# A two-layer transformer on one core: VectorE's exponential from three shifted bit patterns, layer 1's late queries projected in place, another order of its first row blocks

## The chip, the core and the metric

One core of a Trainium2 chip runs the program. It has a matrix engine (TensorE, PE in the profile; its weight loads are PEld), VectorE (DVE), ScalarE (ACT), GpSimd (POOL), and a queue that starts transfers (SyncE, SP). The engines run side by side, each takes its own instructions in order, and they wait for each other by semaphores. Only TensorE, VectorE and ScalarE reach PSUM, the memory into which matmuls write. The metric is the device time of one execution in microseconds; a kernel's time is the median of its runs.

## The reference, cut to what matters

2048 rows of 448 numbers pass twice through the same two blocks, with the same weights: attention with 16 heads of 28, then a hidden layer of 1792 with a squared ReLU.

```python
x = x + A(layernorm(x), wqkv, wo)
x = x + B(layernorm(x), w1, b1, w2, b2)
x = x + A(layernorm(x), wqkv, wo)
x = x + B(layernorm(x), w1, b1, w2, b2)

# A: q, k, v of 16 heads of 28
scores = einsum("bhqd,bhkd->bhqk", q, k) * 28 ** -0.5
o = einsum("bhqk,bhkd->bhqd", softmax(scores), v);  return o @ wo
# B
h = x @ w1 + b1;  r = where(h > 0, h, 0);  return (r * r) @ w2 + b2
```

Softmax needs an exponential for each of 2 x 16 x 2048 x 2048 scores, and its sums come with the product P x V through columns of ones in V.

## The kernel before, in words

**Tiling.** A *unit* is 128 keys' worth of partitions by 512 columns of scores of one head: two key blocks of 128 against a row block of 256 queries (in the last two row blocks four against 128). There are 1024 units in a layer. Four heads make a head group g (four groups), and the eight row blocks (layer 1: nine, the last two of 128 rows) are numbered from 0. A *pass* is one row block, one head group and a range of key blocks; the lists `OPENING` and, in layer 1, `CUTS` and `AHEAD` say in which order passes come.

**Three engines share the exponentials.** TensorE writes scores (L1157) into one of two PSUM tiles of three banks. ScalarE takes all three units of such a tile in one exponential of 128x1536 (L1195), or only two, 128x1024, while VectorE takes the third (`a_unit`, L1219 or L1217). Scores come out scaled so that a unit's value is log2 of the exponential times 128, which is how a bf16 number's bits are spaced. VectorE therefore makes an int16 number out of the score and calls it bits of a bf16 number. In `a_rest` three more operations with constants bend it to the exponential: `bent` (L1266, int16), `half` (L1272, low bytes to f16) and `whole` (L1277, high bytes back in place); the planner gives each to GpSimd or VectorE. `close` (L1281, VectorE) multiplies two of them. The result is the sum of two tiles, `z` and `x2`, and both are multiplied by V on TensorE and added in PSUM (L1383 for `z` and ScalarE's units, L1348 for `x2`). Where much is queued on GpSimd (`PLIM`), another form runs on VectorE alone (`a_whole`, L1235, L1239, L1242).

**Buffers.** ScalarE's results go into a ring of twelve tiles `pt`; VectorE's unit lies in such a tile or in a *cell*: `v_c`, or parts of K, V of a layer that hold nothing yet or nothing more (in rows: `v_c`, `K_sb`, `V_sb`, `h`). Two small PSUM banks (`R_m`) serve everything else: projections, the accumulator of P x V, the hidden layer.

**Order.** The program is written by a `Planner`. Streams (scores, exponentials, P x V, each row block's chain of work) offer their next operation; the planner keeps a clock for each engine, with a duration for each operation, and issues what can start first, by priority. `PACE` holds settings that take effect from the numbered exponential on (`BUSY`, `TB`, `LAG` and so on say when VectorE may take a unit; `HEAT` when a filler matmul, L1644, is put on TensorE); `FORCE` and `SKIP` name exponentials at which VectorE must, or must not, take a unit.

**A row block's chain** (`chain`): output projection, addition to x (L1516), statistics (L651), normalisation (L775), transposes (L715), hidden layer in TensorE (all these projections are L812), ReLU (L1587) and square (L1594), second product, addition (L1516). In layer 0 it goes on to layer 1's keys, values and queries (`qkv`): K of the first two head groups, V, K of the other two, and at once Q (copies from PSUM: L835, L863, L831). In layer 1 the block is stored.

## Time and profile before

| | |
|---|---|
| three runs | 802.92, 803.11, 803.15 us; median 803.11 |
| the profiled execution | span 801.1 us from the first to the last instruction; its page gives no other time of its own |
| instructions | 29158; TensorE 12205 matmuls, VectorE 1836, ScalarE 702, GpSimd 703 |
| ScalarE's exponentials | 683: 344 of 1536 columns, 339 of 1024 |
| opening, exponentials, closing | 0 to 9.3, to 786.5, to 801.1 us |

A row of a group reads: line, engine, operation, written tile <- read tiles, shapes, count | busy time in us, mean duration of one in ns | idle time of the engine just before them, and who ended it. A row of a stretch reads: from:to, its length, then for each engine busy us and instructions, the granted TensorE clock (1.00 is full), the share of the DMA engines, GB/s. A row of the line of time or of the chain reads: start, us, engine, what; a merged row can hold both shapes of a line. A row of waits reads: who waited <- for whom: us in total, times, longest. Busy time of TensorE is modelled, so a busy TensorE is not one at its peak.

### The profile page before, as it was taken

To read this page: it belongs to the slowest core of one execution; us is meant where nothing else is said; L and a number is where in the kernel's file an instruction comes from. 1 tells how busy PE (TensorE), PEld (TensorE's weight loads), DVE (VectorE), ACT (ScalarE), POOL (GpSimd) and SP (SyncE) were. 2 spreads that over 40 slices of the span, in tenths; PEclk is the share of its full clock that TensorE was granted. 3 is DMA by queue.
4 is the path that set the end of the run, shared out by engine and by line. 5 is a ranking of instruction groups with operands and counts; after the bars stand their busy time and mean duration, and the time that the engine had idled before them with its cause. 6 is when DMAs were issued, how large, how long until landed. Compare 5 with 4: busy or idle time off the path is not lost.

```text
span 801.1 us, 29158 instructions
## 1 busy us (share of the span) xinstructions
PE 777.5 (97%) x12205; PEld 417.1 (52%) x12205; DVE 749.9 (94%) x1836; ACT 788.9 (98%) x702; POOL 445.3 (56%) x703
## 2 busy tenths in 40 slices
PE   9999989999999999999999999989999999999998
PEld 6555545544554545555454545445454554445666
DVE  8999999999999999999999998999999999999754
ACT  8999999999999999999999999999999999999995
POOL 3346777657676664544566667767655656533200
PEclk9999999999999999999999999999999999999999
DMA  9200010000000000000000000011100000000000
GB/s 254 82 2 2 4 34 25 17 16 16 17 3 16 16 16 16 3 17 15 2 3 2 2 2 2 12 35 30 32 12 22 21 23 21 27 11 21 22 15 19
DMA packets 32481, 18.13 MB, mean 23 GB/s; under 512 B 17819, under 2 KB 31900, under 8 KB 32349
## 3 DMA queue, kind: packets, MB, share of 16 engines
q1 hardware_dynamic: 32204, 16.16, 7.4%
q8 instruction: 95, 1.56, 0.8%
q14 instruction: 38, 0.30, 0.1%
q10 hardware_dynamic: 144, 0.11, 0.0%
HBM read 13.98 MB, written 2.06 MB: 20 GB/s over the span
## 4 chain that ended last, share of the span: by engine, by line
PE 38%; ACT 36%; DVE 17%; issue 9%; POOL 0%; DMA 0%; ACTq 0%; DVEq 0%
ACT pt L1195 36%; PE mt L812 17%; PE sc L1157 11%; PE oT L1383 6%; DVE pt L1219 2%; DVE r L1587 2%; PE oT L1348 1%; DVE pt L1217 1%; DVE x_sb L1516 1%; DVE st L651 1%; DVE K_sb L1281 1%; DVE v_c L1281 1%; DVE V_sb L1594 1%; DVE oTn L1507 1%; DVE v_c L1219 1%
## 5 line engine op out<-in xcount | busy, mean ns | idle before, releaser
L1195 ACT ACTIVATE pt<-sc 128x1536 bf16<-128x1536 f32 (+1 forms) x683 | 776.1, 1287 | 1.4 <-PE sc L1157 1.1
L1157 PE MATMUL sc<-Q_sb,K_sb 32*128 32x256 bf16 (+1 forms) x4606 | 278.5, 265 | 16.9 <-ACT pt L1195 13.3
L1157 PEld LDWEIGHTS <-K_sb 32*128 32x128 bf16 x4606 | 100.0, 92 | 188.2 <-issue 119.7
L1383 PE MATMUL oT<-pt,V_sb 128*32 128x256 bf16 (+1 forms) x3974 | 168.0, 268 | 0.6 <-DVE Q_sb L831 0.3
L1383 PEld LDWEIGHTS <-V_sb 128*32 128x32 bf16 x4352 | 101.6, 96 | 45.0 <-issue 36.0
L812 PE MATMUL mt<-xnT,w 128*128 128x256 bf16 (+1 forms) x904 | 119.3, 270 | 0.4 <-DVE x_sb L1516 0.2
L1277 POOL TENSOR_SCALAR pt<-pt 128x512 int16<-128x512 int8 x124 | 79.0, 640 | 42.9 <-ACT pt L1195 5.2
L812 PEld LDWEIGHTS <-w 128*128 128x128 bf16 x952 | 78.0, 98 | 34.2 <-issue 25.1
L1219 DVE TENSOR_SCALAR pt<-sc 128x512 int16<-128x512 f32 x128 | 87.3, 685 | 1.9 <-PE sc L1157 1.4
L1587 DVE TENSOR_SCALAR r<-mt 128x512 bf16<-128x512 f32 (+1 forms) x107 | 73.0, 682 | 3.0 <-PE mt L812 2.3
L676 POOL TENSOR_TENSOR rstd<-mv,mhalf 128x2 f32<-128x2 f32 (+1 forms) x34 | 25.4, 747 | 85.1 <-DVE mv L679 58.0
L812 PE MATMUL mt<-w,V_sb 128*128 128x448 bf16 (+2 forms) x288 | 67.2, 346 | 0.0
L1272 POOL TENSOR_SCALAR v_c<-pt 128x512 f16<-128x512 uint8 x55 | 36.5, 665 | 29.6 <-DVE xnT L727 4.6
L1277 POOL TENSOR_SCALAR v_c<-v_c 128x512 int16<-128x512 int8 x60 | 40.2, 670 | 21.0 <-DVE V_sb L1272 4.3
L1219 DVE TENSOR_SCALAR v_c<-sc 128x512 int16<-128x512 f32 x69 | 46.5, 680 | 0.6 <-PE sc L1157 0.6
L1516 DVE TENSOR_TENSOR x_sb<-x_sb,mt 128x448 bf16<-128x448 bf16 x61 | 37.5, 615 | 8.1 <-PE mt L812 7.8
L651 DVE BATCH_NORM_STATS2 st<-x_sb 128x6 f32<-128x448 bf16 x63 | 38.9, 619 | 0.8 <-DMA x_sb<-in_A_x_dram 0.5
L812 PEld LDWEIGHTS <-V_sb 128*128 128x128 bf16 x302 | 25.0, 98 | 24.1 <-issue 10.0
L1348 PE MATMUL oT<-v_c,V_sb 128*32 128x256 bf16 (+1 forms) x306 | 35.7, 272 | 0.0
L1277 POOL TENSOR_SCALAR K_sb<-K_sb 128x512 int16<-128x512 int8 x41 | 26.5, 647 | 10.8 <-DVE v_c L1281 2.4
L1594 DVE TENSOR_TENSOR V_sb<-r 128x512 bf16<-128x512 bf16 x70 | 29.1, 419 | 3.1 <-ACT r L1585 2.8
L812 PE MATMUL mt<-wo,oTn 128*128 128x448 bf16 x128 | 30.3, 355 | 0.4 <-DVE oTn L1465 0.3
(224 smaller groups left out, 1255.9 us busy)
## 6 DMA issues: line engine op xcount, KB each, us to landing
rec<-scr SPq DMA_DIRECT2D x54, 128.0 KB
out_dram<-x_sb SPq DMA_DIRECT2D x15, 112.0 KB
x_sb<-in_A_x_dram SPq DMA_DIRECT2D x7, 224.0 KB
w<-in_B_w_dram SPq DMA_DIRECT2D x1, 1568.0 KB
w<-in_B_w_dram SPq DMA_DIRECT2D x1, 1344.0 KB
dn<-oT_sb SPq DMA_DIRECT2D x54, 4.0 KB
V_sb<-in_A_wqkv_dram SPq DMA_DIRECT2D x4, 168.0 KB
scr<-dn SPq DMA_DIRECT2D x27, 8.0 KB
```

The lines of the kernel that those rows point to most:

```text
L651: nc.vector.bn_stats(out=box["st"][:, :], in_=x_sb[:, t0 + j, :] if src is None else src())
L812: nc.tensor.matmul(box["t"][:, c0:c0 + n], lhsT=lhsT() if callable(lhsT) else lhsT, rhs=rhs, start=a, stop=b)
L1157: nc.tensor.matmul(dst[k][:, i * nt * P:(i + 1) * nt * P], lhsT=K_sb[l][rows, g, (kb + i) * P:(kb + i + 1) * P], rhs=Q_sb[rows, g, t0 * P: ...
L1195: t = nc.scalar.activation(out=pt[:, 0:n], in_=gbuf[gi]["sc"][:, 0:n], func=AF.Exp, scale=float(np.log(2.0)) * 2.0 ** -FRAC)
L1219: t = nc.vector.tensor_scalar(out=z.bitcast(DT.int16), in0=src, scalar1=2.0, scalar2=EXP_BIAS, op0=ALU.mult, op1=ALU.add)
L1272: on(e).tensor_scalar(out=box["f"], in0=gbuf[gi]["z"].bitcast(DT.uint8).rearrange("p (n t) -> p n t", t=2)[:, :, 0], scalar1=2.0 ** -9, sc ...
L1277: on(e).tensor_scalar(out=gbuf[gi]["z"].bitcast(DT.int16), in0=gbuf[gi]["z"].bitcast(DT.int8).rearrange("p (n t) -> p n t", t=2)[:, :, 1], ...
L1348: nc.tensor.matmul(box["t"][DHP * hh:DHP * hh + DHP, 0:n], lhsT=V_sb[l][:, kb + i, 4 * g + hh, :], rhs=gbuf[gi]["x2"][:, i * n:(i + 1) * n ...
L1383: nc.tensor.matmul(box["t"][DHP * hh:DHP * hh + DHP, 0:n], lhsT=V_sb[l][:, tb, 4 * g + hh, :], rhs=p, start=begin and j < G, stop=close an ...
L1516: nc.vector.tensor_tensor(out=x_sb[:, tb, lo:hi], in0=x_sb[:, tb, lo:hi] if src is None else src[:, lo:hi], in1=t[:, 0:hi - lo], op=ALU.add)
L1587: nc.vector.tensor_scalar(out=r[:, 0:w], in0=t[:, 0:w], scalar1=0.0, scalar2=None, op0=ALU.max)
L1594: nc.vector.tensor_tensor(out=h[:, 0:w // n, :], in0=r, in1=r, op=ALU.mult)
```

## The change

**The exponential.** VectorE's first operation now adds one constant to the score and keeps it from going below zero (L1240 after). That int16 number, read as bf16, is a piecewise linear interpolant of the exponential. Two more come from adding 37 and 84 to the same bits (of 128 to an octave; both are `add`, L1261, on GpSimd or VectorE), and VectorE adds these two up (`close`, L1268). `z` is the first tile as it is, `x2` the sum; both are again multiplied by V. `whole`, the operation in place on `z`, and the form on VectorE alone are gone. The ring buffer or cell of `z` is now given back after three readers: both additions and the matmul.

**Late queries.** For row blocks 4 to 7 of layer 0 (`QDEF`), the normalised transposed rows for layer 1 are kept in the place of Q itself. Their Q projections wait until the last keys of layer 1 are there (`late_queries`), and since they overwrite what they read, no result is copied out before the last of the block's projections has run.

**Order of passes.** `BOUND` takes the place of `CUTS`: row blocks 1 to 3 on keys 0 to 9, then row block 0 on keys 0 to 13 and at once 14 and 15, then row blocks 1 to 3 on the rest. Row block 0 is cut once, as before, only later. In layer 0, `OPENING` cuts row block 1's last range in two, keys 8 to 11 and 12 to 15, which adds one sum of partial results (L1408) for each of four head groups.

**Settings.** `PACE` is another table throughout (two rows are shown), and `FORCE` and `SKIP` are part of it. A group of four units (three for ScalarE, one for VectorE) is possible in the code, but `MFREE` of 5 never allows it.

```diff
+SHIFTS = (37, 84)
+def lines(x, by):
+    x = x + by / 2.0 ** FRAC
+    return 2.0 ** np.floor(x) * (1.0 + x - np.floor(x))
+X = np.arange(0.0, 1.0, 2.0 ** -12)
+EXP_BASE = float((127.0 - np.log2(np.mean(sum(lines(X, s) for s in (0, *SHIFTS)) / 2.0 ** X))) * 2.0 ** FRAC)
...
-OPENING = ((0, 0, 2), (0, 2, 4), (1, 0, 4), (1, 4, 8), (0, 4, 8), (0, 8, 12), (1, 8, 16), (0, 12, 16))
+OPENING = ((0, 0, 2), (0, 2, 4), (1, 0, 4), (1, 4, 8), (0, 4, 8), (0, 8, 12), (1, 8, 12), (0, 12, 16), (1, 12, 16))
...
-CUTS = (0, 10, 16)
+BOUND = ((1, 0, 10), (2, 0, 10), (3, 0, 10), (0, 0, 14), (0, 14, 16), (1, 10, 16), (2, 10, 16), (3, 10, 16))
...
-    440: {'HEAT': 0.6, 'WINDOW': 3.4, 'CHUNK': 2},
+    672: {'CHUNK': 3, 'HEAT': 0.6, 'FORCE': (679,)},
...
+            def late_queries():
+                yield Op("-", 0.0, None, deps=[("K", 1, g, NTB - 1) for g in range(G)])
+                for a in qs:
+                    yield from turned(*a, after=[("qq", t0)])
+                yield Op("-", 0.0, None, deps=[last.deps[0]], sets=("qq", t0))
...
         def take(e):
-                t = nc.vector.tensor_scalar(out=z.bitcast(DT.int16), in0=src, scalar1=2.0, scalar2=EXP_BIAS, op0=ALU.mult, op1=ALU.add)
+            t = nc.vector.tensor_scalar(out=z.bitcast(DT.int16), in0=src, scalar1=EXP_BASE, scalar2=0.0, op0=ALU.add, op1=ALU.max)
+        c.need = 3
...
-        t = Op(("POOL", "DVE"), (EDUR, TDUR), bent, deps=[c], acq=lambda: room_for(unit), sets=("t2", gi), port=True)
-        h = Op(("POOL", "DVE"), (EDUR, 0.42), half, deps=[c], acq=lambda: cell_for(unit), port=True)
-        w = Op(("POOL", "DVE"), (EDUR, 0.42), whole, deps=[t, h], sets=("w", gi), port=True)
-        o = Op("DVE", 0.42, close, deps=[t, h], rel=h, sets=("x", gi), port=True)
+        for k in range(2):
+            o.append(Op(("POOL", "DVE"), (EDUR, TDUR), add(o, k), deps=[c], acq=(lambda: cell_for(unit)) if k else (lambda: room_for(unit)),
+                        rel=z, sets=() if k else ("t2", gi), port=True))
+        o = Op("DVE", 0.42, close, deps=ts, rel=ts[1], sets=("x", gi), port=True)
...
-            xt2 = yield from layernorm(t0, nt, None, mv=mv)
+            xt2 = yield from layernorm(t0, nt, None, mv=mv, place=Q_sb[:, :, t0 * P:t0 * P + n] if qb >= QDEF else None)
```

Three places of the built programs show it. First GpSimd, late in layer 0, from one row block's normalisation (`rstd`) on; before:

```order
L676 TENSOR_TENSOR rstd<-mv,mhalf 128x2
L1266 TENSOR_SCALAR K_sb_103<-pt 128x512
L1272 TENSOR_SCALAR v_c<-pt 128x512
L1277 TENSOR_SCALAR pt<-pt 128x512
L1266 TENSOR_SCALAR K_sb_103<-V_sb_106 128x512
L1272 TENSOR_SCALAR v_c<-V_sb_106 128x512
L1266 TENSOR_SCALAR V_sb_106<-v_c 128x512
L1277 TENSOR_SCALAR V_sb_106<-V_sb_106 128x512
L1277 TENSOR_SCALAR v_c<-v_c 128x512
```

Three operations to a unit. The same place now:

```order
L686 TENSOR_TENSOR rstd<-mv,mhalf 128x2
L866 MEMSET V_sb_106 128x16x4
L1261 TENSOR_SCALAR v_c<-pt 128x512
L1261 TENSOR_SCALAR V_sb_106<-v_c 128x512
L1261 TENSOR_SCALAR v_c<-pt 128x512 x2
L1261 TENSOR_SCALAR V_sb_106<-pt 128x512
L1261 TENSOR_SCALAR K_sb_103<-pt 128x512
L1261 TENSOR_SCALAR v_c<-pt 128x512
L1261 TENSOR_SCALAR V_sb_106<-pt 128x512 x2
```

Two operations to a unit, and none that writes where it reads. Second, VectorE where layer 1's last keys come out of PSUM (K_sb_103 holds layer 1's keys); before:

```order
L835 CAST K_sb_103<-mt 128x2x256
L1242 TENSOR_SCALAR V_sb_105<-V_sb_105 128x512
L1266 TENSOR_SCALAR v_c<-K_sb_102 128x512
L1235 TENSOR_SCALAR K_sb_102<-h 128x512
L1239 TENSOR_TENSOR K_sb_102<-h,K_sb_102 128x512
L1408 TENSOR_TENSOR oT_sb<-oT,K_sb_102 128x256
L1219 TENSOR_SCALAR v_c<-sc 128x512
L1281 TENSOR_TENSOR v_c<-v_c,K_sb_102 128x512
L1219 TENSOR_SCALAR v_c<-sc 128x512 x2
L1242 TENSOR_SCALAR h<-h 128x512
L1219 TENSOR_SCALAR K_sb_102<-sc 128x512
L831 TENSOR_SCALAR Q_sb<-mt 128x2x256
```

The last queries follow the last keys. Now the four late blocks' queries stand in pairs behind all keys; the first two pairs:

```order
L841 TENSOR_SCALAR Q_sb<-mt 128x2x256
L1240 TENSOR_SCALAR v_c<-sc 128x512
L841 TENSOR_SCALAR Q_sb<-mt 128x2x256
L1399 TENSOR_TENSOR oT_sb<-oT,K_sb_102 128x256
L1268 TENSOR_TENSOR v_c<-v_c,K_sb_102 128x512
L1268 TENSOR_TENSOR v_c<-v_c 128x512
L1268 TENSOR_TENSOR V_sb_105<-V_sb_105,v_c 128x512
L1479 RECIPROCAL dn<-dn 128x16
L1261 TENSOR_SCALAR v_c<-v_c 128x512 x2
L1240 TENSOR_SCALAR h<-sc 128x512
L841 TENSOR_SCALAR Q_sb<-mt 128x2x256 x2
```

Eight such copies of queries stand behind the last keys instead of two. Third, VectorE at the end of the program (r and V_sb_105: hidden layer; x_sb: the two last row blocks); before:

```order
L727 COPY xnT<-tp 128x4x128
L1594 TENSOR_TENSOR V_sb_105<-r 128x512 x3
L1516 TENSOR_TENSOR x_sb<-K_sb_102,sc 128x448
L1594 TENSOR_TENSOR V_sb_105<-r 128x256
L1516 TENSOR_TENSOR x_sb<-K_sb_102,mt 128x256
L1516 TENSOR_TENSOR x_sb<-K_sb_102,mt 128x192
```

And now:

```order
L737 COPY xnT<-sc 128x4x128
L1578 TENSOR_SCALAR r<-mt 128x256
L1585 TENSOR_TENSOR V_sb_105<-r 128x512 x3
L1585 TENSOR_TENSOR V_sb_105<-r 128x256
L1507 TENSOR_TENSOR x_sb<-K_sb_102,mt 128x256
L1507 TENSOR_TENSOR x_sb<-K_sb_102,sc 128x192
L1507 TENSOR_TENSOR x_sb<-K_sb_102,sc 128x448
```

The addition of row block 7 (128x448) moved behind the two of row block 8.

284 lines of the change are left out of this document (132 added, 152 removed).

## The prediction

> **What bounds the kernel now.** First the page: how busy each engine is, and whether that holds in every slice.
>
> ```profile
> span 801.1 us, 29158 instructions
> PE 777.5 (97%) x12205; PEld 417.1 (52%) x12205; DVE 749.9 (94%) x1836; ACT 788.9 (98%) x702; POOL 445.3 (56%) x703
> ACT  8999999999999999999999999999999999999995
> POOL 3346777657676664544566667767655656533200
> PEclk9999999999999999999999999999999999999999
> ```
>
> ScalarE (ACT) is busy 98% of the span and in every slice but the last; the granted TensorE clock is full throughout. Second, ScalarE's groups with shapes kept apart, and its line of time at both ends.
>
> ```profile
> L1195 ACT ACTIVATE pt<-sc 128x1536 bf16<-128x1536 f32 x344 | 487.6, 1502 | 0.9 <-PE sc L1157 0.8
> L1195 ACT ACTIVATE pt<-sc 128x1024 bf16<-128x1024 f32 x339 | 337.9, 1069 | 0.5 <-PE sc L1157 0.4
> ```
> ```profile
> 9.32 7.08 ACT L1195 ACTIVATE pt<-sc 128x1536 bf16<-128x1536 f32 x5 [0.25 <-PE sc L1157]
> ...
> 769.12 17.39 ACT L1195 ACTIVATE pt<-sc 128x1536 bf16<-128x1536 f32 x13
> ```
>
> The reader is to see one unbroken row of 683 exponentials from 9.32 to 769.12 + 17.39 = 786.51 us, 777.2 us long, with 0.9 + 0.5 = 1.4 us of idle time ahead of them in all. So the time is 9.3 us of opening, 777.2 us of exponentials back to back, and 14.6 us of closing. Inside the row the one lever is how many exponentials are of the short kind, where VectorE takes the third unit: a long one is 1502 ns and a short one 1069 ns, and the difference, 433 ns, is what a unit costs on ScalarE. Third, the other engines by stage.
>
> ```profile
> core 0: us, PE busy (x) PEld busy (x) DVE busy (x) ACT busy (x) POOL busy (x), PEclk, DMA share, GB/s
> 80.00:120.00 40.00, 38.09 (x580) 20.70 (x572) 38.80 (x91) 40.00 (x37) 29.96 (x47) 1.00 0.08 18
> 512.00:532.00 20.00, 17.48 (x295) 8.34 (x294) 19.52 (x51) 20.00 (x20) 12.19 (x19) 1.00 0.13 31
> 720.00:760.00 40.00, 39.41 (x851) 23.93 (x843) 35.40 (x85) 40.00 (x34) 12.81 (x19) 1.00 0.07 19
> 760.00:786.50 26.50, 26.16 (x626) 16.58 (x614) 14.21 (x36) 26.50 (x21) 1.82 (x2) 1.00 0.09 20
> 786.50:801.10 14.60, 11.53 (x153) 9.38 (x150) 6.45 (x18) 4.94 (x10) 1.67 (x2) 0.98 0.06 17
> ...
> 798.40:801.10 2.70, 0.00 (x0) 0.00 (x0) 0.32 (x1) 0.00 (x0) 0.00 (x0) 0.90 0.15 43
> ```
>
> VectorE is at 97% to 98% in the middle, so it can take more units only if a unit costs it less. In the closing TensorE works 11.53 of 14.6 us, and 2.7 of the other 3.1 lie behind its last matmul: what the change adds to TensorE there is added to the time.
>
> **The change part by part.** Durations are those of the profiled execution, whose span is 801.1 us; the median of the three runs, 803.11 us, lies 2.0 us above it. I add those 2.0 us unchanged.
>
> *The exponential.* The order of the two programs gives the counts. Short exponentials go from 339 to 352, long ones from 344 to 331; together they stay 683. So 13 units leave ScalarE: 13 x 433 ns = 5.6 us. What a unit costs the other two engines:
>
> ```profile
> L1219 DVE TENSOR_SCALAR pt<-sc 128x512 int16<-128x512 f32 x128 | 87.3, 685 | 1.9 <-PE sc L1157 1.4 <-issue 0.2
> L1281 DVE TENSOR_TENSOR v_c<-v_c 128x512 bf16<-128x512 bf16 x58 | 24.3, 420 | 1.1 <-POOL v_c L1272 1.1
> L1266 DVE TENSOR_SCALAR v_c<-pt 128x512 int16<-128x512 int16 x21 | 6.0, 285 | 0.0
> L1277 DVE TENSOR_SCALAR v_c<-v_c 128x512 int16<-128x512 int8 x9 | 3.8, 419 | 0.0
> L1277 POOL TENSOR_SCALAR pt<-pt 128x512 int16<-128x512 int8 x124 | 79.0, 640 | 42.9 <-ACT pt L1195 5.2
> L1266 POOL TENSOR_SCALAR v_c<-pt 128x512 int16<-128x512 int16 x29 | 19.7, 680 | 11.7 <-DVE pt L1219 3.8 <-DVE oTn L1507 2.6 <-DVE V_sb L1594 1.1
> L1408 DVE TENSOR_TENSOR oT_sb<-oT,K_sb 128x256 f32<-128x256 f32 x20 | 8.3, 416 | 0.3 <-PE oT L1383 0.2
> ...
> L1348 PE MATMUL oT<-v_c,V_sb 128*32 128x256 bf16 x294 | 34.9, 274 | 0.0
> ```
>
> Every new operation has a row of its own form already: the conversion from PSUM (685 ns), the add of a constant in int16 (285 ns on VectorE, 680 on GpSimd), the closing sum (as the product, 420). VectorE: conversions and closings go from 338 to 351, 13 x (685 + 420) = +14.4 us; int16 constants on VectorE from 124 + 68 + 68 = 260 to 211, 49 x 285 = -14.0; the byte forms, 46 x 419 = -19.3, are gone; partial sums of P x V go from 37 to 41 (row block 1's new cut in layer 0), 4 x 416 = +1.7. Sum -17 us of 749.9. GpSimd: 640 operations at 640 to 680 ns become 491 at 680, some 640 x 650 - 491 x 680 = -82 us of 445.3. TensorE: 13 more units have a second tile to multiply with V, two 256-column matmuls of 274 ns each, 7.1 us even if none ran beside another, spread over the whole span; and 30 filler matmuls (31 before, one now) go. All of this lies beside the exponentials, so I cost it at nothing. Its cover is the row of exponentials itself; should a conversion come late, the next scores can't be written and ScalarE waits, and that is priced below.
>
> *Layer 1's late queries and the new order of row blocks.* The projections are the same in number and size (1366 matmuls of 256 columns and 721 of 448 in both orders), only later, and no DMA is added or moved past another. For row blocks 4 to 7 the evacuation of the first pair of head groups waits on VectorE for the last matmul of the second, and behind it in VectorE's order stand the next conversions. Both small PSUM banks are held until then, so P x V, later on TensorE, can't open its accumulator; its lag is taken up by the twelve buffers of exponentials. Below, this costs 0 as long as a buffer is free; above, it is the rival on the ring. I take 0, since the nearest rows, those of the exponentials, show 1.4 us of idle time in all, with queries and P x V already competing for these banks. The last keys' copies now stand at the 436th and 439th exponential (429th and 435th before); by the list of passes their first scores are due about the 439th, so one of them may cost up to a step, 1.1 us: that is in the range.
>
> *The closing.* Here the order differs to the chip's cost. After the last score matmul TensorE has eight more 128x448 matmuls of the second product (two rows of its order each: 375 rows for 359), and it ends on six of row block 7's, so a whole 448-column addition and a 112 KB store end the program instead of a 192-column one with 48 KB.
>
> ```profile
> 789.62 1.51 PE sc L812 x8
> 791.13 0.23 PE tp L715 x4
> ...
> 793.01 2.25 PE mt L812 x40
> ```
> ```profile
> 791.19 0.92 PE L812 MATMUL sc<-w,V_sb 128*128 128x448 bf16 x4
> 791.95 1.06 PE L812 MATMUL sc<-xnT,w 128*128 128x128 bf16 x16
> ```
> ```profile
> 795.80 0.61 DVE L1516 TENSOR_TENSOR x_sb<-K_sb,sc 128x448 bf16<-128x448 f32 x1
> ...
> 798.36 0.35 DVE L1516 TENSOR_TENSOR x_sb<-K_sb,mt 128x192 bf16<-128x192 f32 x1 [0.68 <-PE mt L812]
> ```
> ```profile
> 0.72 2.51 DMA x_sb<-in_A_x_dram
> ```
>
> Eight matmuls: 1.51 us (the row with x8). The last row block's hidden layer starts at 791.95, 0.59 us after its transposes end (791.13 + 0.23); four matmuls of the second product cover that now, and afterwards only two of 128 columns stand there, 2 x 2.25 / 40 = 0.11 us: +0.48. The last addition: 0.61 - 0.35 = +0.26. The store: from the end of the addition, 798.71, to the end of the span, 801.1, is 2.4 us for 48 KB, and a 112 KB load took 2.51, so between 0 and +0.5; I take +0.2, nearer the small end, as a store of 48 KB and a load of 112 took nearly the same. Sum +2.4 us.
>
> The opening is the same instruction by instruction through the first 24 exponentials: 0. Together -5.6 + 2.4 = -3.2 us: a span of 797.9 and a time of **799.9 us**.
>
> [...] Between the 454th and the 458th exponential TensorE's new order holds scores alone, with no P x V, no projection and no filler.
>
> ```profile
> L1644 PE MATMUL mt<-xn,ident x31: 349/362/364, 117.7 to 728.5; 128*128 128x448 bf16 x31
> ```
> ```profile
> 523.58 0.40 PE L1157 MATMUL sc<-Q_sb,K_sb 32*128 32x256 bf16 x6
> ...
> 527.01 0.61 PE L1157 MATMUL sc<-Q_sb,K_sb 32*128 32x256 bf16 x12 [0.20 <-DVE v_c L1219]
> ```
>
> A group of scores is 0.40 us and an exponential's step 777.2 / 683 = 1.14, so TensorE works 35% of these five steps, where the row from 512 to 532 us has 17.48 of 20 with filler in it, at a clock of 1.00. No row shows what 35% does. [...]
>
> **The rivals.**
>
> *More than the sum.* VectorE and GpSimd have 17 and 82 us less to do, and score matmuls wait for VectorE now:
>
> ```profile
> PEld L1157 <- DVE pt L1219: 5.5, 18, 0.6
> PEld L1157 <- DVE v_c L1219: 3.8, 11, 0.7
> PEld L1157 <- DVE v_c L1281: 3.6, 14, 0.4
> ```
>
> These three rows are 12.9 us. If a fifth of that reaches ScalarE's start times today and goes, 2.6 us more are won: 797.3. Against it: the order is packed again with 13 more units, so the relief is partly spent.
>
> *The clock falls at the bridge.* Suppose a fall to a half that lasts as long as the thin stretch, 5 x 1.14 = 5.7 us. TensorE, at 17.48 / 20 = 87% there, has 5.0 us of work in it, needs 9.9 at half clock, and ends some 4.3 us late; between nothing of that (the buffers take it up) and all of it reaches ScalarE, 799.9 to 804.2, in the middle 802.0: no difference that could be told. For it: the thin stretch. Against: a group of scores at half clock, 0.80 us, still fits into a step of 1.14.
>
> *The ring of twelve is full (slower).* An exponential writes into the buffer of the one twelve before it. In the order of before there are 9 exponentials whose buffer is last read by a P x V that stands on TensorE behind the scores of its next user; now there are 24, since P x V runs later. If ScalarE waits there for one more chunk of P x V,
>
> ```profile
> 215.06 0.99 PE oT L1383 x32
> ```
>
> which for 16 matmuls is half of 0.99, 0.5 us, the 15 new places cost 7.5 us: 807.4. It decides from 3.2 / 15 = 0.21 us a place. Against it: at the 9 places of before ScalarE's idle time totals no more than the 1.4 us above.
>
> **How the numbers follow.** The forecast gets 0.50 (its own range 798.0 to 801.4: the store's bound, and a microsecond of waits either way), more than the sum 0.20, the clock 0.14, the ring 0.16. A difference under 0.2%, 1.6 us, is about what a measurement of this kernel can't tell from none; so faster is below 801.5: 0.50 + 0.20 = 0.70. The clock is "the same", 0.14, the ring slower, 0.16. The range leaves half of the ring's chance above and a small part of the second case below: 796.5 to 804.5.
>
> **What the profile after would show.** Right: 331 long and 352 short exponentials with idle time under 3 us, their row some 771.6 us long from 9.3 us on; VectorE near 733 us busy, GpSimd near 363; a closing of 17 us with TensorE ending on row block 7's second product. The ring: ScalarE waiting for a P x V or for its buffer around the 24 places, above all every eleventh exponential. The clock: a granted clock under 1.00 near 520 us. The prediction is wrong if conversions on VectorE come late all along, which would lengthen the row of exponentials without any one large wait.

## The result, and the profile after

The changed kernel takes 807.62 us (median of four runs, 807.24 to 808.40) where the kernel before, beside it, takes 803.13 us (802.92 to 803.19): a ratio of 1.0057, 95% interval 1.0043 to 1.0071. It is slower by 4.5 us; 799.9 us had been forecast, 7.7 us less. First the page of the profile after, the same lines as were shown of before:

```profile
span 805.8 us, 29069 instructions
PE 779.5 (97%) x12187; PEld 417.2 (52%) x12187; DVE 744.5 (92%) x1771; ACT 786.3 (98%) x702; POOL 359.6 (45%) x554
PEclk9999999999999999999999999989999999999999
```

GpSimd is about as busy as forecast (359.6 us for 363), VectorE is not: 744.5 us for 733. And one digit of the granted clock is an 8. Then ScalarE's exponentials by shape, from its groups of instructions:

```profile
L1220 ACT ACTIVATE pt<-sc 128x1536 bf16<-128x1536 f32 x331 | 476.7, 1488 | 1.4 <-PE sc L1182 0.7 <-ACT pt L1220 0.2
L1220 ACT ACTIVATE pt<-sc 128x1024 bf16<-128x1024 f32 x352 | 356.7, 1065 | 3.1 <-PE sc L1182 1.6 <-DVE K_sb L1261 0.3 <-DVE K_sb L1397 0.3
```

The counts are the forecast ones, 331 and 352, so 13 units did leave ScalarE. But the idle time ahead of the exponentials is 1.4 + 3.1 = 4.5 us, where it was 1.4. ScalarE's line of time shows where the row breaks (a row ends where the engine stood idle for a moment; start, us, engine, what, and in brackets the idle time ahead of the first):

```profile
9.33 7.07 ACT L1220 ACTIVATE pt<-sc 128x1536 bf16<-128x1536 f32 x5
16.94 117.14 ACT L1220 ACTIVATE pt<-sc 128x1536 bf16<-128x1536 f32 x103 [0.53 <-PE sc L1182]
134.34 217.69 ACT L1220 ACTIVATE pt<-sc 128x1024 bf16<-128x1024 f32 x192 [0.27 <-PE sc L1182]
352.24 38.50 ACT L1220 ACTIVATE pt<-sc 128x1536 bf16<-128x1536 f32 x34 [0.20 <-PE sc L1182]
391.09 25.76 ACT L1220 ACTIVATE pt<-sc 128x1024 bf16<-128x1024 f32 x23 [0.35 <-PE sc L1182]
417.10 41.98 ACT L1220 ACTIVATE pt<-sc 128x1024 bf16<-128x1024 f32 x39 [0.25 <-DVE K_sb L1397]
459.36 28.12 ACT L1220 ACTIVATE pt<-sc 128x1024 bf16<-128x1024 f32 x26 [0.28 <-DVE K_sb L1261]
487.65 44.89 ACT L1220 ACTIVATE pt<-sc 128x1024 bf16<-128x1024 f32 x40 [0.18 <-PE sc L1182]
533.02 20.91 ACT L1220 ACTIVATE pt<-sc 128x1024 bf16<-128x1024 f32 x18 [0.48 <-PE sc L1182]
554.28 13.71 ACT L1220 ACTIVATE pt<-sc 128x1024 bf16<-128x1024 f32 x12 [0.34 <-PE sc L1182]
568.22 219.19 ACT L1220 ACTIVATE pt<-sc 128x1536 bf16<-128x1536 f32 x191 [0.23 <-ACT pt L1220]
```

The row runs from 9.33 to 568.22 + 219.19 = 787.41 us, 778.1 us. Forecast were 771.6, and before it was 777.2. Of the 5.5 us of ScalarE's work that left the row, less than nothing is won.

The merged rows hide waits shorter than the ones they break at. So I add up, over the 682 intervals from one exponential's start to the next, what lies above the shortest step of its shape (1.330 us after a long one, 0.904 after a short one; 13 x 0.426 = 5.5 us is the units' price by these steps). I call this *the waits of the row*. The same sum for each kernel, in parts by the number of the exponential (waits, end of the row and closing are those of the one profiled execution, the median is that of all runs; `e2_late_add`'s profiled execution took 805.2 us, 1.4 us less than its median; the kernels are explained in the next section):

| kernel | 0-439 | 440-499 | 500-682 | waits, us | end of the row | closing | median, us | ratio to before (95%) |
|---|---|---|---|---|---|---|---|---|
| before | 8.9 | 1.1 | 3.0 | 13.0 | 786.50 | 14.6 | 803.1 | |
| after | 12.2 | 3.1 | 4.2 | 19.5 | 787.41 | 18.4 | 807.6 | 1.0057 (1.0043-1.0071) |
| e1_fill | 11.8 | 2.8 | 4.2 | 18.9 | 786.69 | 18.4 | 807.1 | 1.0049 (1.0034-1.0064) |
| e2_late_add | 11.8 | 1.9 | 4.2 | 18.0 | 785.77 | 17.6 | 806.6 | 1.0044 (1.0028-1.0061) |
| e9_fill_late | 11.8 | 1.1 | 4.2 | 17.2 | 785.04 | 17.6 | 805.2 | 1.0027 (1.0017-1.0036) |
| e6_noclose | 8.8 | 2.4 | 4.2 | 15.4 | 783.32 | 18.4 | 804.2 | 1.0013 (1.0004-1.0023) |
| e15_all | 8.3 | 1.1 | 4.2 | 13.7 | 782.23 | 17.6 | 801.6 | 0.9983 (0.9974-0.9993) |
| e7_pv | 11.3 | 3.0 | 3.0 | 17.3 | 785.39 | 18.2 | 804.8 | 1.0019 (1.0009-1.0028) |
| e16_pool | 8.7 | 2.5 | 3.6 | 14.8 | 782.74 | 18.4 | 802.3 | 0.9993 (0.9983-1.0002) |
| e17_rows | 9.5 | 2.6 | 4.2 | 16.3 | 784.07 | 18.3 | 804.6 | 1.0022 (1.0013-1.0032) |

Against the forecast, the row is 778.1 - 771.6 = 6.5 us too long, which is just the waits' growth from 13.0 to 19.5, and the closing 18.4 - 17.0 = 1.4 us. Three places stand out.

*Spread over the whole row*, waits grew by 3.3 us up to the 440th exponential and 1.2 behind the 500th. (0.40 us of the 3.3 is one wait, at the exponential 108. No other run of this order has it, not even those whose edits stand far behind that place, so it is of this one execution.) What TensorE's matmuls stood idle for before the products of P x V (its two lines after, then the `z` line of before; before, there was no such wait at all ahead of the `x2` products):

```profile
its engine sat idle before it (us, times) until:
  DVE v_c L1268: 0.4, 2
  DVE K_sb L1268: 0.2, 1
```
```profile
its engine sat idle before it (us, times) until:
  DVE oT_sb L1399: 1.0, 3
  DVE Q_sb L841: 0.3, 1
  DVE r L1578: 0.2, 1
  DVE x_sb L1507: 0.2, 1
```
```profile
its engine sat idle before it (us, times) until:
  DVE oT_sb L1408: 0.4, 1
  DVE Q_sb L831: 0.3, 1
  DVE K_sb L835: 0.2, 1
```

TensorE's matmuls now stand idle nine times, 2.3 us, for VectorE's closing sum, its partial sums, a copy of queries, its ReLU and its additions; before, they did three times, 0.9 us. The scores of the next exponential stand behind these products in the order of the program. These idle times, all over 0.15 us, are less than what the waits grew by, so they show where VectorE is late but not that this is all of it; for that the experiments were made.

*At 524 to 536 us* the clock fell (stretches: from:to, length, then busy us and instructions of TensorE, its loads, VectorE, ScalarE, GpSimd; granted clock; DMA). The last row is the closing, and below stand two of TensorE's rows from the stretch's line of time:

```profile
524.00:528.00 4.00, 2.03 (x42) 1.37 (x42) 4.00 (x12) 4.00 (x5) 0.00 (x0) 1.00 0.12 38
528.00:532.00 4.00, 3.96 (x37) 1.47 (x34) 3.55 (x10) 3.80 (x4) 0.97 (x2) 0.51 0.12 31
532.00:536.00 4.00, 4.00 (x68) 2.12 (x66) 3.14 (x6) 3.37 (x4) 1.03 (x2) 0.64 0.02 6
787.41:805.80 18.39, 13.63 (x168) 10.37 (x166) 7.93 (x19) 4.83 (x10) 1.59 (x2) 1.00 0.06 20
```
```profile
525.36 0.61 PE L1182 MATMUL sc<-Q_sb,K_sb 32*128 32x256 bf16 x12 [0.52 <-ACT pt L1220]
526.70 0.40 PE L1182 MATMUL sc<-Q_sb,K_sb 32*128 32x256 bf16 x6 [0.73 <-ACT pt L1220]
```

In the thin stretch TensorE worked 2.03 of 4 us (3.23 in the same 4 us of the kernel before), never idle for more than 0.73 us at a time. The clock is at half behind it, for 6.8 us (means of 0.51 and 0.64 in the next two stretches), and ScalarE, which had been busy all along, stands idle 0.20 and 0.63 us there.

*In the closing* VectorE, GpSimd and TensorE in this order (line of time):

```profile
791.83 1.17 DVE L785 TENSOR_SCALAR xn<-x_sb,mv,rstd 128x448 bf16<-128x448 bf16 x1
```
```profile
791.84 1.03 POOL L1549 TENSOR_TENSOR K_sb<-x_sb,K_sb 128x448 f32<-128x448 bf16 x1
```
```profile
793.05 0.40 PE L725 MATMUL sc<-ident,xn 128*128 128x128 bf16 x4 [1.14 <-DVE xn L785]
```

The last rows' normalisation takes 1.17 us where the mean of its line was 398 ns before, at the very moment of GpSimd's bias addition (L1549), and TensorE waits 1.14 us for it. Before, that addition began 0.16 us behind the normalisation, which took 0.39 us, and the addition itself 1.12.

### The profile page after: what moved, and what is told of

Its sections match the earlier page's. It is cut to its first block, busy times and chain, and to the rows that moved or that the text cites. A ratio compares the mean times of both kernels' runs of the same rounds, so it can differ in the third digit from the quotient of the medians.

```text
span 805.8 us, 29069 instructions
## 1 busy us (share of the span) xinstructions
PE 779.5 (97%) x12187; PEld 417.2 (52%) x12187; DVE 744.5 (92%) x1771; ACT 786.3 (98%) x702; POOL 359.6 (45%) x554
## 4 chain that ended last, share of the span: by engine, by line
PE 39%; ACT 25%; DVE 25%; issue 8%; DMA 2%; POOL 0%; SPq 0%; ACTq 0%; DVEq 0%; POOLq 0%
ACT pt L1220 25%; PE mt L822 17%; PE sc L1182 11%; PE oT L1374 7%; DVE pt L1240 6%; PE oT L1339 2%; DVE v_c L1268 2%; DVE r L1578 2%; DVE x_sb L1507 2%; DVE st L661 2%; DMA rec<-scr 1%; DVE V_sb L1268 1%; DVE v_c L1240 1%; PE sc L822 1%; DVE K_sb L1268 1%
## 5 line engine op out<-in xcount | busy, mean ns | idle before, releaser
L1182 PE MATMUL sc<-Q_sb,K_sb 32*128 32x256 bf16 (+1 forms) x4586 | 278.2, 266 | 15.2 <-ACT pt L1220 11.8
L1261 POOL TENSOR_SCALAR v_c<-pt 128x512 int16<-128x512 int16 x150 | 99.5, 664 | 119.6 <-DVE pt L1240 62.4
L1240 DVE TENSOR_SCALAR pt<-sc 128x512 int16<-128x512 f32 x216 | 146.6, 682 | 2.3 <-PE sc L1182 1.7
L1374 PEld LDWEIGHTS <-V_sb 128*32 128x32 bf16 x4352 | 101.3, 96 | 46.1 <-issue 42.9
L1261 POOL TENSOR_SCALAR K_sb<-pt 128x512 int16<-128x512 int16 x87 | 59.0, 678 | 58.2 <-DVE pt L1240 28.1
L822 PE MATMUL mt<-w,V_sb 128*128 128x448 bf16 (+1 forms) x274 | 66.4, 351 | 0.0
L1261 POOL TENSOR_SCALAR V_sb<-pt 128x512 int16<-128x512 int16 x77 | 50.9, 661 | 34.7 <-DVE pt L1240 13.2
L1339 PE MATMUL oT<-v_c,V_sb 128*32 128x256 bf16 (+1 forms) x334 | 41.8, 273 | 0.7 <-DVE v_c L1268 0.4
L1240 DVE TENSOR_SCALAR v_c<-sc 128x512 int16<-128x512 f32 x54 | 36.7, 681 | 1.3 <-PE sc L1182 1.0
L1268 DVE TENSOR_TENSOR v_c<-v_c 128x512 bf16<-128x512 bf16 x79 | 35.2, 449 | 1.1
L1339 PEld LDWEIGHTS <-V_sb 128*32 128x32 bf16 x722 | 26.6, 96 | 14.1 <-issue 13.1
L1240 DVE TENSOR_SCALAR K_sb<-sc 128x512 int16<-128x512 f32 x45 | 30.7, 683 | 1.3 <-PE sc L1182 1.1
```

Of the source, the lines that this page charges most:

```text
L822: nc.tensor.matmul(box["t"][:, c0:c0 + n], lhsT=lhsT() if callable(lhsT) else lhsT, rhs=rhs, start=a, stop=b)
L1182: nc.tensor.matmul(dst[k][:, i * nt * P:(i + 1) * nt * P], lhsT=K_sb[l][rows, g, (kb + i) * P:(kb + i + 1) * P], rhs=Q_sb[rows, g, t0 * P: ...
L1240: t = nc.vector.tensor_scalar(out=z.bitcast(DT.int16), in0=src, scalar1=EXP_BASE, scalar2=0.0, op0=ALU.add, op1=ALU.max)
L1261: (nc.vector if e == "DVE" else nc.gpsimd).tensor_scalar(out=box[at_].bitcast(DT.int16), in0=gbuf[gi]["z"].bitcast(DT.int16), scalar1=1.0, ...
L1268: nc.vector.tensor_tensor(out=box[0], in0=box[0], in1=box[1], op=ALU.add)
L1339: nc.tensor.matmul(box["t"][DHP * hh:DHP * hh + DHP, 0:n], lhsT=V_sb[l][:, kb + i, 4 * g + hh, :], rhs=gbuf[gi]["x2"][:, i * n:(i + 1) * n ...
```

## The experiments

In all of them the order of instructions is that of the kernel named, except for what the diff says. An experiment that undid the late queries or the new order of row blocks alone isn't among them: the planner then packs all the rest differently, so that it would not have told the one part.

### The arithmetic alone, in the old order

Before's order with the new operations in the old places (cut; the lines on `bent` and `half` are in words, and `whole` does nothing). The 68 units that ran on VectorE alone keep their mask step as second term:

```diff
-scalar1=2.0, scalar2=EXP_BIAS, op0=ALU.mult, op1=ALU.add          # conversion
+scalar1=EXP_BASE, scalar2=0.0, op0=ALU.add, op1=ALU.max
-bent: z * 0.5 + EXP_ONE;  half: low bytes * 2**-9 + 0.5;  whole: high bytes in place
+bent: z + 37;             half: z + 84 (int16)
-nc.vector.tensor_tensor(..., op=ALU.mult)                         # close
+nc.vector.tensor_tensor(..., op=ALU.add)
```

> Kernel before, its order of instructions and its split of the units between ScalarE and VectorE kept, with the new exponential put into the places of the old one: the conversion adds a bias, the two GpSimd steps become integer additions of 37 and 84 and the closing multiplication an addition. The few units that ran on VectorE alone keep their one mask step as their second term, so that this kernel's output is not the exponential's sum there. Theory A (the new arithmetic by itself is neither faster nor slower, and all of the change's effect comes from how many units each engine gets and in which order): exponential row within 0.5 us of 777.2 us, time 802.5 to 804.0 us. Rival (the additions on GpSimd or VectorE are dearer than the steps which they replace, and VectorE is late because of it): waits of the exponential row grow as in the changed kernel, by 3 to 6 us, time 806 to 809 us.

803.12 us, ratio 1.0000 (0.9990 to 1.0009); the waits are 13.0 us, the closing 14.6. In the old order and with the old split the new exponential costs and gains nothing, although GpSimd is busy 287 us instead of 445 and VectorE 739 instead of 750. What the change does to the time comes from how many units go where and in which order.

### The 13 units given back

Cut to what matters:

```diff
+insides[0] += gbuf[gi]["in"]
+gbuf[gi]["back"] = gbuf[gi]["in"] and insides[0] % 16 == 0 and insides[0] <= 208
...
+n += 512 * gbuf[gi]["back"]          # ScalarE's exponential takes the unit again
```

> Changed kernel, its order kept, with 13 of VectorE's units (every 16th of those that lie beside ScalarE's own scores) given back to ScalarE as 512 more columns of the same exponential; their conversion, additions, closing sum and the second of their two products are left out, and the first product takes ScalarE's result. Long exponentials 331 + 13 = 344, short 339, as in the kernel before. Theory A (ScalarE's row is still the wall, and the 13 units did take 13 x 433 ns off it, which the waits gave back): row + 5.6 us less what the waits near these units lose, time 811 to 813.2 us. Rival (VectorE or TensorE has become the wall, so that ScalarE's work has slack): the waits of the row shrink by as much as the work grows, time 806.5 to 809 us.

811.03 us, ratio 1.0100 (1.0085 to 1.0115): 3.4 us more than the changed kernel. Of the units' 5.5 us, 3.4 show in the medians. In the profiled executions the waits took up 1.3: they fell from 19.5 to 18.2 us, although the edit makes a new one of 1.3 us at the exponential 348. ScalarE's row was still the wall, theory A just above its lower bound. It also says what the new order costs at most: with before's split of 344 and 339 it is 7.8 us slower than before's order, of which 4.1 are the longer closing (18.7 us) and 1.3 the new wait.

### The clock and the closing

```diff
+if 452 <= gi <= 458:                  # e1; e9: if 455 <= gi <= 458: again = max(again, 1)
+    again = max(again, 2)             # issue these scores again
...
+tc.add_manual_dep(add.ins, norm_at[t0].ins.name, ...)     # e2 and e9: L1549 waits for xn
```

> Changed kernel with one edit: the score matmuls of the exponentials 452 to 458 are issued three times instead of once to three times (the repeats write the same scores again), so that TensorE does not stand idle in the thin stretch at 524-528 us; the order is otherwise the same. Theory A (the fall of the granted clock at 528.06-534.91 us costs the waits at the exponentials 459-465 and 480, 2.0 us between 440 and 500 beyond those of before): granted clock 1.00 in every window from 500 to 560 us, exponential row 2.0 us shorter, time 807.6 - 2.0 = 805.6 us. Rival (those waits come from VectorE being late, and the low clock only coincides with them): the clock stays up, the waits stay, 807.6 us; a third outcome is that the repeats only move the thin stretch, and the clock falls elsewhere.

> Changed kernel with one edit: GpSimd's addition of the bias to the residual of the last rows (L1549, 1.03 us) waits for the normalised rows xn, as it came after them in the kernel before. Theory A (the two ran at the same moment and slowed each other, xn 1.17 us beside 0.39 before): xn takes about 0.4 us again, the gap of TensorE ahead of the last hidden tile falls from 1.14 to about 0.4 us, closing 17.6 us instead of 18.4, time 806.8 us. Rival (the added rows then come late, or another wait stands behind the first): xn is short, but the closing stays at 18.4 us and the time at 807.6 us.

> Changed kernel with both small repairs together: GpSimd's late bias addition waits for xn, and the scores of the exponentials 455 to 458 are issued twice (18 matmuls more, which fits into the 2.0 us in which TensorE stood idle between 523.1 and 527.4 us, where the heavier repeat of seven exponentials had itself made the exponentials 453 and 454 wait 1.3 us). Theory A (the clock's fall costs 2.0 us and the repeats cost nothing where TensorE is idle; the closing gains 0.8 us): granted clock 1.00, row 2 us shorter, time 804.8 us. Rival (of the waits after the clock's fall most belong to the order of TensorE's work there): clock 1.00, but the row gains only about 0.7 us, as with the heavier repeat, time 806.1 us.

With seven exponentials' scores repeated the clock was 1.00 in all runs, but the time fell only to 807.09 us: the exponentials 453 and 454 now wait 0.88 and 0.41 us, beside the repeats. The late addition brought 806.59 us and the closing of 17.6 us that theory A gave. Both together, with a lighter repeat, are 805.24 us. The same stretch, and then normalisation, addition and transposes, of that kernel:

```profile
524.00:528.00 4.00, 2.69 (x57) 1.89 (x59) 3.97 (x13) 4.00 (x4) 0.00 (x0) 1.00 0.11 39
```
```profile
789.46 0.40 DVE L785 TENSOR_SCALAR xn<-x_sb,mv,rstd 128x448 bf16<-128x448 bf16 x1
```
```profile
790.00 1.04 POOL L1552 TENSOR_TENSOR K_sb<-x_sb,K_sb 128x448 f32<-128x448 bf16 x1 [0.57 <-DVE xn L785]
```
```profile
789.91 0.40 PE L725 MATMUL sc<-ident,xn 128*128 128x128 bf16 x4 [0.37 <-DVE xn L785]
```

TensorE works 2.69 of 4 us in the thin stretch, the clock stays at 1.00, and the waits between the 440th and the 500th exponential are those of before, 1.1 us instead of 3.1. xn takes 0.40 us, and TensorE waits 0.37. So the clock cost 2.0 us of the row and the collision 0.8 us of the closing. The runs of this kernel scatter with their mean clock: those at 1.000 took 804.4 to 805.0 us, those at 0.996, where it fell all the same, 806.3 and 806.4 us.

### Is VectorE late, or has TensorE too much to do?

The two edits are made one at a time, and both leave the order as it is:

```diff
-nc.vector.tensor_tensor(out=box[0], in0=box[0], in1=box[1], op=ALU.add)
+nc.vector.tensor_tensor(out=box[0][:, 0:64], in0=box[0][:, 0:64], in1=box[1][:, 0:64], op=ALU.add)   # e6, e15
...
+kept[0] += 1                                                   # e7, and e8 on before
+if kept[0] % 5 == 0 and not begin and not close: continue      # leave out a step of P x V
```

> Changed kernel, its order kept, but the closing sum of VectorE's units (L1268) works on 64 of the 512 columns, so that the third interpolant is left out of most of the output. It takes most of 343 x 0.42 us off VectorE and the product of such a unit finds its operand ready sooner. Theory A (VectorE is late: TensorE stands in order before the product of VectorE's unit, and the scores queued behind it come late, at the exponentials 108, 300, 334, 357, 396, 422 and 480, 3.06 us of waits together, and in many smaller ones): these waits go, the waits of the exponential row fall from 19.5 to about 15 us, time 803 to 804.6 us. Rival B (TensorE's own amount of work or the bare order of its instructions makes the scores late): waits stay at 18 to 20 us, time 806.5 to 807.6 us.

> Changed kernel, its order kept, with 432 of its 5074 matmuls of the product P x V left out (each fifth step that neither opens nor closes a group), so that the output lacks these keys: about 19 us less of TensorE's 759 us beside the exponentials, spread over the whole stretch. Theory B (TensorE's amount of work is the wall together with ScalarE's, and with 13 units fewer ScalarE catches up with it): the waits of the row fall from 19.5 to below 14 us, time 802 us or less. Rival A (VectorE is late): the waits stay within 2 us of 19.5, time 805.5 to 807.6 us, since the products that wait for VectorE still wait. Rival C (the waits come from single places in the order, where one long piece of TensorE's work stands ahead of the scores, and not from the amount): they fall in proportion to the work left out, by some 1 to 3 us.

> Kernel before with the same edit as the changed kernel's with a fifth of the steps of P x V left out (408 of 5042 matmuls, some 18 us of TensorE). Theory B (TensorE's amount of work makes the difference): waits of the row from 13.0 to about 10 us, time 800 us, and the changed kernel with this edit is then no slower than this one, since its 13 units fewer (5.6 us) show. Rivals A and C: the waits change by less than 2 us, time 801 to 803 us, and the changed kernel stays 3 us or more behind.

The short closing sum gives 804.20 us, 3.4 us less. ScalarE's line of time:

```profile
9.32 7.07 ACT L1220 ACTIVATE pt<-sc 128x1536 bf16<-128x1536 f32 x5
16.93 508.59 ACT L1220 ACTIVATE pt<-sc 128x1536 bf16<-128x1536 f32 x454 [0.53 <-PE sc L1182]
525.93 3.70 ACT L1220 ACTIVATE pt<-sc 128x1024 bf16<-128x1024 f32 x3 [0.41 <-PE sc L1182]
529.88 34.01 ACT L1220 ACTIVATE pt<-sc 128x1024 bf16<-128x1024 f32 x30 [0.25 <-PE sc L1182]
564.12 219.20 ACT L1220 ACTIVATE pt<-sc 128x1536 bf16<-128x1536 f32 x191 [0.23 <-ACT pt L1220]
```

From 16.93 to 525.5 us it has no break at all, where the changed kernel had six; the waits at the exponentials 300, 334, 357 and 422 are under 0.1 us, at 396 it is 0.15 (the one at 108 is absent without the edit too). The clock fell here as well (0.50 from 524 to 528 us), and the 1.2 us behind the 500th exponential stay.

But less work on TensorE gains nearly as much: 432 matmuls of P x V less gave 804.75 us, 2.9 us, waits 19.5 to 17.3, and in the kernel before 802.75 us, 0.4 us, 12.6 for 13.0. Theory B falls in the form in which it was stated: the waits stay far above 14 us, and the changed kernel with that edit is still 2.0 us behind. Theory A's range for this edit, 805.5 us or more, was missed as well; what fits is the third outcome, 1 to 3 us of waits in proportion to the work left out. So TensorE's work is not the wall by itself, but in the new order it counts, and VectorE's lateness alone doesn't explain the waits.

> Kernel before with the closing product of its VectorE units on 64 of 512 columns, as the changed kernel had its closing sum shortened (most of the output lacks the quadratic part of the exponential). Theory A (that VectorE is late for TensorE is a matter of the changed kernel's order): the waits of the row, 13.0 us, fall by less than 1.5 us, time 801.8 to 803 us, against 4.1 us which the same edit took off the changed kernel's row. Rival F (any kernel of this kind gains as much from a lighter VectorE): row 3 to 4 us shorter, time 799 to 800 us.

> Changed kernel with both small repairs and the closing sum on 64 of 512 columns (most of the output lacks the third interpolant). Theory A (three separate causes that add up: VectorE's lateness 3.4 us, the clock 1.4 to 2 us, the closing 0.8 to 1.0 us): 807.6 - 3.4 - 2.4 = 801.8 us, below the kernel before by more than 0.1%, granted clock 1.00. Rival (the causes overlap, since the thin stretch is itself made by a late VectorE): 803 us or more.

The same short sum in the kernel before (`close` of both forms) gives 802.32 us, 0.8 us less, waits 12.2 for 13.0. So the loss that a shorter closing sum cures belongs to the changed order. And the changed kernel with all three causes taken away, short sum, repeats and late addition:

```profile
9.99 6.80 ACT L1222 ACTIVATE pt<-sc 128x1536 bf16<-128x1536 f32 x5
17.14 545.66 ACT L1222 ACTIVATE pt<-sc 128x1536 bf16<-128x1536 f32 x487 [0.34 <-PE sc L1184]
563.04 219.19 ACT L1222 ACTIVATE pt<-sc 128x1536 bf16<-128x1536 f32 x191 [0.24 <-ACT pt L1222]
```

801.58 us, ratio 0.9983 (0.9974 to 0.9993): the causes add up, 3.4 + 2.4 = 5.8 us forecast from the single runs, 6.0 measured. Its row is 772.2 us long, where 771.6 were forecast, with 13.7 us of waits for 13.0 before. It starts 0.7 us later and ends 4.3 us earlier than before's, and the closing is 3.0 us longer. So the row's forecast gain is there once the three causes are gone; of the 3.2 us of time that were forecast, 1.5 show, in a kernel that leaves out most of its closing sums.

### Moving the products instead

In 19 places (e12: ahead of exponentials that waited over 0.15 us) or all 136 (e13), a product of VectorE's unit is issued behind the next scores. Both start from `e9_fill_late`, 805.24 us (cut):

```diff
+if held or begin or close or not zs or not (scored[0] + 1 in MOVED):
+    flush(); go()
+else:
+    held.append(go)          # issued behind the next score matmuls
```

> Changed kernel with the two small repairs (bias addition behind xn, scores of 455 to 458 twice; 805.24 us), and in it, at 19 places where TensorE stood in order before a product of VectorE's unit and the next exponential waited over 0.15 us, that product is put behind the next scores instead of ahead of them. Nothing is left out. Theory A (TensorE stands in order behind VectorE's late operands): the waits at the exponentials 300, 334, 357, 396 and 422, 2.0 us together, and half of the smaller ones go; row 2 to 3 us shorter, time 802.3 to 803.3 us. Rival D (where VectorE is late, it is late for its next conversion too, and the scores then wait for their bank instead): the waits move to the next exponentials, time 804.5 to 805.3 us.

> The same with every product of VectorE's units that neither opens nor closes a group put behind the next scores, 136 places. Theory A: as many waits go as at the 19 places, and of the many under 0.15 us some more; time 801.5 to 803 us. Rival E (a score group waits for its bank more often than a product for VectorE, so that a product put behind it comes late and TensorE loses more than it gains): waits of the row grow, time 806 us or more.

805.35 us for 805.24: the waits at 396 and 422 went, 0.84 us, and new ones came, 0.70 us at 416 and 0.28 at 301. Everywhere, 808.70 us and waits of 21.1 us. Rivals D and E hold: here a late operand isn't cured by letting TensorE do something else first, the waits move on to later exponentials. Which step carries them there isn't shown.

### What makes VectorE late

Three edits of the changed kernel, `e18_to_pool` again starting from `e9_fill_late`, and the first of them in the kernel before (cut):

```diff
+if e == "POOL":                                           # e16, and e19 on before
+    nc.gpsimd.memset(box[at_].bitcast(DT.uint32), 0)      # instead of the addition
+    return
...
+n = 64 if s_left else hi - lo                             # e17: additions to x_sb, and bn_stats
...
-(nc.vector if e == "DVE" else nc.gpsimd).tensor_scalar(   # e18
+(nc.vector if e == "DVE" and turns[0] % 4 else nc.gpsimd).tensor_scalar(
```

> Changed kernel, its order kept, with GpSimd's additions of 37 and 84 (some 480 of 0.66 us) replaced by a fill of the same tile with zero, which is shorter and does not wait for the conversion; the shifted terms that GpSimd makes are so left out. VectorE's work is the same as in the changed kernel. Theory G (the chain of a unit is late on GpSimd, 0.66 us where the order was made for 0.617 us, and the closing sum and the product wait for it): the waits at 300, 334, 357, 396, 422 and 480 go as with the shortened closing sum, row 3 to 4 us shorter, time 803.5 to 804.5 us. Rival V (VectorE has more to do than fits ahead of each product, and GpSimd has time to spare): waits change by less than 1.5 us, time 806 to 807.6 us.

> Changed kernel, its order kept, with VectorE's work lightened by about as much as by the shortened closing sum (some 50 to 60 us), but in work that is no part of a unit's chain: the additions to the residual x_sb and the batch statistics of the rows take 64 of 448 columns while exponentials run, so that the rows' sums and moments are left incomplete. Theory V (VectorE's amount of work makes it late): waits fall from 19.5 to 15 to 16.5 us as with the shortened closing sum, time 803.5 to 805 us. Rival W (only the closing sum's own length, 0.42 us directly ahead of the product, was on TensorE's path): waits fall by less than 2 us, time 805.8 to 807.6 us.

> Changed kernel with the two small repairs (805.24 us), and each fourth of VectorE's own additions of 37 and 84 given to GpSimd in the same place of the order (0.66 us on GpSimd for 0.29 us on VectorE; 34 of them). Nothing is left out. Theory V (VectorE is late, GpSimd has time): about 10 us less on VectorE, a sixth of what the shortened closing sum took off, row 0.5 to 0.7 us shorter, time 804.5 us. Rival X (the additions were given to VectorE because their sums were urgent, and on GpSimd they come 0.4 us later): new waits, time 805.5 to 807 us.

> Kernel before with the same edit as the changed kernel whose GpSimd additions were replaced by fills (0.32 us instead of 0.66 us, no wait for the conversion): its some 600 steps on GpSimd are filled with zero, so that the terms which GpSimd makes are left out. Theory H (in the kernel before the products already stood far enough behind VectorE's units, so that a shorter chain gains it little; the changed kernel's order has them closer): waits of the row fall from 13.0 by less than 1.5 us, time 801.5 to 803 us, against 4.7 us of waits and 5.3 us of time in the changed kernel. Rival J (GpSimd's work costs any order of this kernel as much): waits fall by 4 us or more, time 797.5 to 799.5 us.

With fills in place of GpSimd's additions the changed kernel takes 802.27 us, 5.3 us less, more than theory G had (803.5 to 804.5). Part of that is the clock, whose mean was under 0.998 in three of these ten runs and in all four of the changed kernel: at means of 0.993 and 0.995 it took 802.9, 803.4 and 804.9 us, where the changed kernel took 807.2 to 808.4 at 0.993 to 0.996. At a like clock, then, some 4 us. VectorE is then busy 734.9 us instead of 744.5, though it has the same operations. The closing sum's largest group and GpSimd's largest, after and then in this experiment:

```profile
L1268 DVE TENSOR_TENSOR v_c<-v_c 128x512 bf16<-128x512 bf16 x79 | 35.2, 449 | 1.1
```
```profile
L1261 POOL TENSOR_SCALAR v_c<-pt 128x512 int16<-128x512 int16 x150 | 99.5, 664 | 119.6 <-DVE pt L1240 62.4 <-DVE V_sb L1261 8.7 <-DVE v_c L1261 7.9
```
```profile
L1271 DVE TENSOR_TENSOR v_c<-v_c 128x512 bf16<-128x512 bf16 x79 | 32.4, 413 | 1.1
```
```profile
L1262 POOL MEMSET v_c<- 128x256 uint32 x223 | 68.8, 319 | 225.0 <-DVE pt L1240 47.2 <-DVE v_c L1264 22.2 <-DVE K_sb L1264 16.5
```

The sum falls from 449 to 413 ns in this group, and from 430 to 412 in the mean of all its groups. Off the chain, 29 us less of VectorE's work (744.5 to 715.3; the expectation had 50 to 60) gave 804.56 us, waits 16.3: theory V. So both count in the new order, the amount of VectorE's work and the chain through GpSimd. Giving more of the chain to GpSimd made it worse, 811.06 us for 805.24, beyond rival X's 807: 52 additions moved (I had written 34), and the closing sum waits for GpSimd. The same group there:

```profile
L1272 DVE TENSOR_TENSOR v_c<-v_c 128x512 bf16<-128x512 bf16 x79 | 35.5, 453 | 4.0 <-POOL v_c L1265 3.3
```

In the kernel before, fills for GpSimd's 640 steps gave 802.90 us, ratio 0.9996 (0.9987 to 1.0006), waits 12.7 for 13.0. The chain is no bound there.

What the same kind of edit gains in each order, us (each against its kernel's own median):

| edit | changed order | order before |
|---|---|---|
| closing on 64 of 512 columns (e6, e14) | 3.4 | 0.8 |
| fills for GpSimd's steps (e16, e19) | 5.3, some 4 at a like clock | 0.3 |
| a fifth of the steps of P x V left out (e7, e8) | 2.9 | 0.4 |
| additions to x and statistics on 64 of 448 columns (e17) | 3.1 | not run |

Lighter work on any of the three engines gains 3 to 4 us in the one order and, where it was run, under 1 in the other. That shows the order as the cause, with the split of units that belongs to it, and not which engine's lateness comes first in it. Order and split aren't told apart: with the 13 units given back and without that edit's own wait, 10.3 us of waits are left up to the 440th exponential, against 11.8 (without the one at 108) and 8.9 before.

## Why the prediction was wrong, point by point

**The price of a unit on ScalarE** was right: the counts are as forecast, 13 units are 5.5 us by the steps of the row, and giving them back cost 3.4 us of time, a new wait of 1.3 us among them.

**"All of this lies beside the exponentials, so I cost it at nothing"** is the step that failed, and the largest: 3.3 us of new waits up to the 440th exponential, which the short closing sum takes away, and perhaps the 1.2 behind the 500th, which it doesn't. I summed VectorE's and GpSimd's work and found less of it (-17 and -82 us), and took the cover of ScalarE's row as given. I wrote that a late conversion "is priced below", but none of the rivals priced one that comes later than before. What a score waits for isn't a sum of work: it is how far ahead of it the other engines' results stand in the order. In the order before there is room: shortening the closing product gained 0.8 us, fills for GpSimd's steps 0.3, fewer products 0.4. In the new one there is little: the same edits gained 3.4 us, some 4 and 2.9. My last sentence named the sign (conversions late all along, no single large wait), but no rival had it. "More than the sum" had the sign wrong. Its three rows were of weight loads, which run beside matmuls (417.1 us of loads and 777.5 of matmuls in a span of 801.1): all such loads ahead of scores waited 62 us for VectorE before and 61 after, so they tell nothing of this loss.

**VectorE's sum itself** was right as a sum and was read against the wrong figure. The durations of all VectorE's instructions, added up, fell by 17.7 us, from 883.8 to 866.1. The page's busy time counts a moment once, and neighbouring VectorE instructions overlap in the record, by 133.9 us in all before and 121.6 after: 65 instructions fewer overlap less, so busy time fell by only 5.4. The closing sum is no large part of it: 430 ns in the mean of all its groups, where before's closing products took 425 and I had 420. With additions on GpSimd its largest group takes 449 ns, and 413 with fills there. The additions read a tile and take 0.66 us; the fills only write one and take 0.32 us. Which of these differences shortens the sum isn't shown. Nor is it shown that this slowing, and not the additions' length or their wait for the conversion, is what made the chain late: the experiment changed all three (a conversion ended 62.4 of the 119.6 us of idle time ahead of the additions' largest group, and 47.2 of the 225.0 us ahead of the fills').

**The clock** fell as the second rival had it, at the place named, to a half, for 6.8 us. I had given 4.3 us as its most and 2.1 as the middle; 2.0 us of the row is what it cost. I had made it a rival to the forecast, with a chance of 0.14, where it was a term that came on top of the others. That it falls to a half, and that a group of six score matmuls then takes twice its time, 0.80 us, was my assumption: the trace after shows the half (0.50 from 528.06 to 534.91 us), but 0.61 us for each of the groups at 528.13, 529.22 and 530.38 us, where those at full clock take 0.40. TensorE's longest idle time in the stretch before the fall was 0.73 us; no idle time and no share of work at which the clock falls comes out of the runs (see the last section).

**The ring of twelve** fell: at its 24 places the waits are 1.6 us together, 0.07 a place where it needed 0.21. Of the two largest, the one at 300 goes with the shorter closing sum, and the one at 108 is of one execution. The rival was also misdescribed: in the order of the two programs the P x V stands at these places behind the scores of the exponential before the buffer's next user. Behind that user's own scores it stands in one place before and in none after, so the ring could hardly add to the scores' own lateness.

**The late queries** and the new order of row blocks, costed at nothing, can't be judged by themselves. TensorE waited 0.3 us for Q (L841) ahead of P x V, as before (L831). What they and the new table make together, the new order, costs up to 7.8 us with before's split, closing included.

**The closing**, +2.4 forecast, was +3.8: the collision of xn with L1549, 0.8 us, was not in my list, since I counted matmuls there and not which instructions of VectorE and GpSimd meet; TensorE's own work grew by 13.63 - 11.53 = 2.1 us where I had 1.5. The last addition (0.62 us) and the store's +0.2 were as forecast.

The sum: 799.9, + 6.5 us of waits (2.0 of the clock, 3.3 up to the 440th exponential, and 1.2 behind the 500th that aren't attributed), + 1.4 of the closing, makes 807.8, within 0.2 us of the measured 807.62.

Open is why the new order leaves so little room, and which engine's lateness comes first: VectorE's, GpSimd's and TensorE's work all count in it. Both programs give the planner the same durations for an addition on GpSimd and for the closing, and the change's parts can't be put in one by one without packing all of it anew.

## What to carry to other kernels

When two engines are nearly always busy (here TensorE 97% and ScalarE 98% of the span) and others feed them, removing work from the wall pays only as far as the others' results arrive in time in the new order; ask for each consumer how long ahead its operand is ready, since the sum of the work doesn't tell. To test it, make one engine's work shorter and keep the order, in both kernels. Edits that gain 3 to 4 us in the one and under 1 in the other name the order as the cause; to name an engine, an edit on another one must gain nothing, which wasn't so here. Moving the consumers only moved the waits. Compare sums of durations with sums of durations, and busy time with busy time. And when a change drops fillers, price the clock as a term of the sum (here 2.0 us), not as another outcome.
